# Summing the logit weights in four column groups, ordering the last two steps by hand, and idle matmuls in the last chain

## The chip, the cores and the metric

One NeuronCore of a Trainium2 chip runs the whole program. The metric is the device time of one execution in microseconds (us); the median of three executions stands in the table below. The engines are named as in the profile: PE (TensorE matmuls), PEld (TensorE weight loads), DVE (VectorE), ACT (ScalarE), POOL (GpSimd) and SP (the queue that issues the loads).

## What is computed

Three layers in a row, all in float32:

```python
attn = chunk_attention(q, k, v, mem_k, mem_v)        # 4 batches, 8 heads, 768 tokens, head size 64
x    = attn.reshape(3072, 512)
h    = x @ w_in                                      # 3072 x 2048
g    = (a0 + a1*h + a2*h^2 + a3*h^3) / (1 + |b0|*|h| + |b1|*h^2 + 1e-6)
x    = g @ w_out                                     # 3072 x 512
logits     = x @ phi                                 # 3072 x 32 slots
slot_input = softmax(logits, over tokens).T @ x      # 32 x 512, 4 slots for each of 8 experts
slot_out   = relu(slot_input[e] @ w1[e]) @ w2[e]     # each expert: 512 -> 1024 -> 512
out        = softmax(logits, over slots) @ slot_out  # 3072 x 512
```

## The kernel before

**The algebra.** `x = g @ w_out` is never formed. The logits are `g @ (w_out @ phi)`, and the kernel first makes the "logit weights" `wp = w_out @ phi` (2048 x 32). The slot input is `(softmax.T @ g) @ w_out`, so `w_out` is used once more at the end.

**Blocks and steps.** The 3072 tokens are 6 blocks of 512; a block has 8 steps of 256 features of `h`, so there are 48 steps, numbered `kk` (`total` is 48). A step's operations are written as letters in lists (`KN`), and `run_step(kk, what)` (line 558) issues one of them:

- `h0`, `h1`: the matmuls of step kk+1, two halves of 128 features by 512 tokens into a PSUM tile `h` of two banks (line 349). Block 0 multiplies in full float32; the later blocks in three products of a faster type.
- `a1`: ACT makes |b0 h| (line 576), |b1| h^2 (577) and a3 h + a2 (579); DVE adds the first two into the denominator `s` (578). `d1`: POOL refines the reciprocal of the step before (`refine`, line 553, q times w), DVE goes on with the numerator `t` (589, 590). `a2`: ACT makes a first reciprocal `w` of the denominator by Ln and Exp (595, 596). `t`: DVE finishes the step before (606, 607), which gives its `g` tile.
- `p0`, `p1`: `post` for a step two back. It turns the `g` tile on PE (line 375) and ACT copies it out of PSUM (376); in every second step `lg` accumulates the logits of two steps from `wp` (368, four column groups of 32).
- `x1` to `x3`: the softmax of a finished block (`soft1`, `soft2`, `soft3`, lines 382 to 436): the sum of the four column groups by the matrix `stack` (386, 389), maxima and Exp, the turn of the weights (416), and the product with the turned `g` tiles into `u_acc` (426, 431).
- `w1`, `z1` (block 0 alone): `wp_chunk` (line 438) turns 256 rows of `w_out` by PE and copies them out of PSUM by ACT (448) and DVE (446); `wp_sum` (line 450) makes two feature tiles of `wp` from them: for each of two tiles four matmuls over the chunks of 128 columns, with the turned `w_out` as weights (128 columns) and `phi` as the moving operand (32 columns), accumulated in PSUM (line 455), then one ACT copy (456).

The attention of block b+1 runs in slices (`at`) between the steps of block b. Block 0 also narrows `w_in` and `w_out` from their 64 bit form (`f64_narrow`, lines 300 to 304, on ACT and DVE).

**The last two steps.** Step 46 runs by the list `ordl`, step 47 by `ordz`. In step 47 the helper `parts` cuts each elementwise operation into two halves of 512 elements, so that its `g` tile comes out in halves; `refine` is on POOL there too. Two more passes (kk = 48, 49) turn the last `g` tiles; then come `soft1` to `soft3` of block 5, the turn of `u_acc` (655), the product with `w_out` (662), the sum of four groups (670), the experts' first product (683), its Relu and turn (689 to 699), the second product (720, 728) and the output.

**What sets the order.** The engines' queues are laid out by a scheduler from the order of the program and its own costs, except inside `tc.manual_schedule(engines=...)`, where the named engines keep the order that is written. `tc.issue_after(ins)` queues what its block issues behind `ins` on that engine. A queue runs strictly in order. Tiles come from pools with a fixed number of buffers: `p_S` and `p_T` (5 each, of 128 x 1024), `p_s2` (one buffer, tag "s2"), `ps_m` (three PSUM banks, taken by `bank`), `ps_h` (two tiles of two banks). A buffer is taken again when its last reader is done.

**The loads at the end.** SP loads the experts' weights (`fill`, line 536, 512 KB each) into whatever buffers come free: those of `xt` after the matmuls of step 47, those of `p_T` and `p_S` after the last steps, those of `p_g` after `soft3` of block 5, that of `p_v` after the first experts' matmuls that read it.

## Time and profile before

| | us |
|---|---|
| median of three executions | 587.33 |
| all three | 587.33, 587.27, 592.0 |
| the profiled execution | 591.32 |
| its span, first to last instruction | 589.5 |
| PE busy | 547.0 (93% of the span) |
| DVE busy | 451.8 (77%) |
| ACT busy | 413.8 (70%) |
| POOL busy | 124.3 (21%) |
| mean granted TensorE clock | 0.971 of full |

All rows come from the profiled execution, which ran about 4 us longer than the median. A busy PE is not PE at its peak, since the ends of matmuls are modelled; matmuls start one behind the other, and the distance of their starts tells what one costs. Times in the rows are us from the start of the span.

### The profile page before, as it was taken

What the parts mean: (1) busy time and instruction counts of PE and PEld (TensorE: products, weight loads), DVE (VectorE), ACT (ScalarE), POOL (GpSimd) and SP (SyncE); (2) the same over time, 40 slices, a digit from 0 to 9 for tenths busy, and PEclk for the clock granted to TensorE, in tenths of its full rate; (3) what the DMA queues carried; (4) which work ended last, traced back from release to release, by engine and by line L of the source; (5) the groups of instructions that cost most, each with busy time, mean ns of one, the idle gap of its engine ahead of it and who ended that gap; (6) DMA issues with size and microseconds to landing.
All of it is one profiled execution on the core that took longest, in us unless ns stands there. A gap on an engine that the chain in (4) does not pass through costs nothing.

```text
span 589.5 us, 13536 instructions
## 1 busy us (share of the span) xinstructions
PE 547.0 (93%) x5880; PEld 376.9 (64%) x5880; DVE 451.8 (77%) x565; ACT 413.8 (70%) x534; POOL 124.3 (21%) x65
## 2 busy tenths in 40 slices
PE   5699999999999999999999999999999999679991
PEld 5565655657767777677766777776778577237351
DVE  3668998988998989878798698896887868920132
ACT  1479997879887978769687778686888878620132
POOL 0010322212231313312231313131322333400000
PEclk9599998999999999999999999999999999898996
DMA  8879775320234312221021022210365224979949
GB/s 353 349 285 387 289 240 213 116 100 1 108 108 143 101 47 108 73 92 60 30 109 73 3 106 74 108 43 31 109 216 213 108 107 143 368 291 349 411 184 359
DMA packets 21371, 97.41 MB, mean 165 GB/s; under 512 B 2624, under 2 KB 2752, under 8 KB 16320
## 3 DMA queue, kind: packets, MB, share of 16 engines
q1 hardware_dynamic: 20160, 92.35, 42.1%
q0 software_dynamic: 1152, 4.19, 1.9%
q8 instruction: 46, 0.75, 0.5%
q14 instruction: 13, 0.11, 0.1%
HBM read 86.05 MB, written 10.49 MB: 164 GB/s over the span
## 4 chain that ended last, share of the span: by engine, by line
PE 65%; DVE 15%; ACT 10%; issue 5%; POOL 2%; DMA 1%; SPq 0%; ACTq 0%; DVEq 0%; POOLq 0%
PE h L349 32%; PE m L375 4%; PE m L426 4%; PE lg L368 3%; ACT S L576 3%; PE h L683 3%; PE m L225 2%; ACT g L376 2%; ACT S L577 2%; PE lg L720 2%; DVE T L589 2%; DVE S L578 2%; PE m L455 2%; PE m L243 2%; DVE T L590 2%
## 5 line engine op out<-in xcount | busy, mean ns | idle before, releaser
L349 PE MATMUL h<-xt,win 128*128 128x512 f32 x1024 | 268.9, 411 | 0.7 <-DVE T L590 0.6
L349 PEld LDWEIGHTS h<-xt,win 128*128 128x128 f32 x1024 | 186.1, 188 | 48.5 <-issue 10.0
L553 POOL TENSOR_TENSOR S<-S,S 128x1024 f32<-128x1024 f32 (+1 forms) x49 | 117.3, 2395 | 305.9 <-DVE S L578 287.8
L576 ACT ACTIVATE S<-h,ctab 128x1024 f32<-128x1024 f32 (+1 forms) x49 | 53.8, 1099 | 55.2 <-PE h L349 53.8
L578 DVE SCALAR_TENSOR_TENSOR S<-S,S 128x1024 f32<-128x1024 f32 (+1 forms) x49 | 58.7, 1199 | 40.4 <-ACT S L577 40.2
L606 DVE SCALAR_TENSOR_TENSOR T<-T,ctab,S 128x1024 f32<-128x1024 f32 (+1 forms) x49 | 64.8, 1324 | 0.0
L589 DVE TENSOR_TENSOR T<-T,h 128x1024 f32<-128x1024 f32 (+1 forms) x49 | 58.3, 1190 | 7.2 <-ACT T L579 7.2
L375 PEld LDWEIGHTS m<-ident,T 128*128 128x128 f32 x384 | 44.0, 143 | 30.6 <-issue 17.1
L590 DVE SCALAR_TENSOR_TENSOR T<-T,ctab,h 128x1024 f32<-128x1024 f32 (+1 forms) x49 | 61.3, 1251 | 0.8
L607 DVE SCALAR_TENSOR_TENSOR T<-S,T 128x1024 f32<-128x1024 f32 (+1 forms) x49 | 59.1, 1206 | 2.0
L579 ACT ACTIVATE T<-h,ctab 128x1024 f32<-128x1024 f32 (+1 forms) x49 | 59.2, 1208 | 0.0
L595 ACT ACTIVATE S<-S 128x1024 f32<-128x1024 f32 (+1 forms) x49 | 51.7, 1055 | 7.1 <-DVE S L578 4.9
L596 ACT ACTIVATE S<-S,ctab 128x1024 f32<-128x1024 f32 (+1 forms) x49 | 55.8, 1138 | 1.0
L376 ACT ACTIVATE g<-m 128x512 f32<-128x512 f32 x96 | 53.3, 602 | 3.4 <-PE m L375 3.2
L375 PE MATMUL m<-ident,T 128*128 128x128 f32 x384 | 53.5, 280 | 1.6 <-DVE a L186 1.6
L577 ACT ACTIVATE S<-h,ctab 128x1024 f32<-128x1024 f32 (+1 forms) x49 | 54.2, 1106 | 0.6 <-DVE T L606 0.6
L368 PE MATMUL lg<-T,wp 128*32 128x512 f32 x192 | 34.6, 612 | 4.9 <-DVE T L607 4.9
L349 PE MATMUL h<-xt,x 128*128 128x512 f32 x64 | 33.0, 635 | 0.0
L187 ACT ACTIVATE a<-a 128x512 f32<-128x512 f32 x22 | 13.7, 639 | 18.5 <-DVE a L186 18.5
L336 POOL DMA_DIRECT2D wo<-win x8 | 5.3, 666 | 84.1 <-DVE win L304 75.7
L426 PE MATMUL m<-g,s 128*32 128x512 f32 x192 | 21.8, 595 | 0.4 <-ACT s L418 0.4
L302 ACT ACTIVATE g<-g 128x1024 f32<-128x1024 f32 x16 | 18.6, 1170 | 3.5 <-DVE g L301 3.5
(172 smaller groups left out, 644.7 us busy)
## 6 DMA issues: line engine op xcount, KB each, us to landing
win<-in_moe_w_dram SPq DMA_DIRECT2D x32, 512.0 KB, 5.5
k<-in_kw_dram SPq DMA_DIRECT2D x11, 1024.0 KB, 6.0
v<-in_vw_dram SPq DMA_DIRECT2D x11, 1024.0 KB, 6.3
g<-in_moe_w_in_dram SPq DMA_DIRECT2D x8, 1024.0 KB, 7.2
g<-in_moe_w_out_dram SPq DMA_DIRECT2D x8, 1024.0 KB, 8.2
out_dram<-win SPq DMA_DIRECT2D x12, 512.0 KB, 5.0
q<-in_qw_dram SPq DMA_DIRECT2D x11, 512.0 KB, 3.6
wo<-win POOLq DMA_DIRECT2D x8, 512.0 KB, 7.7
```

The source lines that it names most:

```text
L349: PE.matmul(tile_[:, f2, :], lhsT=ww[:, c, f2 * P:f2 * P + P], rhs=xx[:, c, :], start=(n == 0), stop=(n == len(pairs) * NC - 1))
L375: PE.transpose(pb[:, m, f2 * P:f2 * P + P], t_[:, f2, tt * P:tt * P + P], ident)
L376: ACT.activation(gts[b, qd][:, 2 * part:2 * part + 2, 2 * P * o:2 * P * o + 2 * P], pb, AF.Copy)
L553: POOL.tensor_tensor(out[:, o], q[:, o], w[:, o], ALU.mult)
L576: ACT.activation(s[:, o], hh[:, o], AF.Abs, scale=b0)
L577: ACT.activation(y[:, o], hh[:, o], AF.Square, scale=rb1)
L578: DVE.scalar_tensor_tensor(s[:, o], y[:, o], QC, s[:, o], ALU.add, ALU.add)
L579: ACT.activation(t[:, o], hh[:, o], AF.Identity, bias=a2, scale=a3)
L589: DVE.tensor_tensor(t[:, o], t[:, o], hh[:, o], ALU.mult)
L590: behind[kk] = DVE.scalar_tensor_tensor(t[:, o], t[:, o], a1, hh[:, o], ALU.add, ALU.mult).ins
L606: DVE.scalar_tensor_tensor(t[:, o], t[:, o], a0, w[:, o], ALU.add, ALU.mult)
L607: DVE.scalar_tensor_tensor(t[:, o], e[:, o], 2.0, t[:, o], ALU.subtract, ALU.mult, reverse0=True)
```

## The change

Three things. First, `wp_sum` makes one product for each of the four chunks of 128 columns, with `phi` as weights (32 columns) and the turned `w_out` as moving operand (256 columns for two feature tiles), each into its own 32 PSUM partitions; ACT copies that to a tile of the pool `p_s2`; two matmuls with `stack` as moving operand then sum the four groups and turn the result in one. Second, the list `ordz` and the helper `parts` go, and `last_steps` writes out steps 46 and 47 for ACT, DVE and POOL by hand: the refinement of step 46 is cut into two halves on POOL, that of step 47 is on DVE, the finish of step 46 stands behind the first part of step 47, and the ACT copies of step 45's turned tile stand between the two halves of Ln and Exp. Third, `keep_busy` issues matmuls of the identity with itself (128 x 128 float32) into a PSUM tile that nobody reads, queued behind given matmuls: 5 in `soft1`, 2 in `soft3`, 19 in `last_steps` (the last 7 read `w`), 2 after the turn of `u_acc`, 3 after the product with `w_out`.

```diff
-    'ordz': "d0 a1 t d1 a2 p0 p1".split(),
     'ordl': "a1 h0 d1 t a2 x2 h1 p0 p1 x1 x3".split(),
 }
 
@@ -372,7 +371,7 @@
         for m in range(2):
             for f2 in range(2):
                 tt = 2 * part + m
-                PE.transpose(pb[:, m, f2 * P:f2 * P + P], t_[:, f2, tt * P:tt * P + P], ident)
+                st["turn"] = PE.transpose(pb[:, m, f2 * P:f2 * P + P], t_[:, f2, tt * P:tt * P + P], ident)
         ACT.activation(gts[b, qd][:, 2 * part:2 * part + 2, 2 * P * o:2 * P * o + 2 * P], pb, AF.Copy)
         if part and o:
             del gt_tile[k - 1], gt_tile[k]
@@ -386,7 +385,9 @@
         PE.matmul(lt, lhsT=stack, rhs=lgs, start=True, stop=True)
         ct = bank([P, TT, NSLOT])
         for tt in range(TT):
-            PE.matmul(ct[:, tt, :], lhsT=lgs[:, tt * P:tt * P + P], rhs=stack[:, 0:NSLOT], start=True, stop=True)
+            done = PE.matmul(ct[:, tt, :], lhsT=lgs[:, tt * P:tt * P + P], rhs=stack[:, 0:NSLOT], start=True, stop=True)
+        if b == NBLK - 1:
+            keep_busy(done.ins, 5)
         old, neg_m = (run[:, n:n + 1] for n in ((2, 0) if b % 2 else (0, 2)))
         bm, db = p_sm("bm", [P, 1]), p_sm("db", [P, 1])
         DVE.tensor_reduce(bm, lt, AX.X, ALU.max)
@@ -432,7 +433,9 @@
         for j in range(4):
             del gts[b, j]
         pb = bank([P, P])
-        PE.transpose(pb, ce.rearrange("p t s -> p (t s)"), ident)
+        done = PE.transpose(pb, ce.rearrange("p t s -> p (t s)"), ident)
+        if b == NBLK - 1:
+            keep_busy(done.ins, 2)
         ACT.activation(c_all[:, b, :], pb, AF.Copy)
 
     def wp_chunk(i):
@@ -448,11 +451,15 @@
                 ACT.activation(ws[:, j], pb, AF.Copy)
 
     def wp_sum(i):
+        ws = wos.pop(i)
+        pb = bank([P, 2, P])
+        for c in range(NC):
+            PE.matmul(pb[32 * c:32 * c + 32], lhsT=phi_sb[:, c, :], rhs=ws[:, :, c, :], start=True, stop=True)
+        part = p_s2("s2", [P, 2, P])
+        ACT.activation(part, pb, AF.Copy)
         pb = bank([P, 2, NSLOT])
-        ws = wos.pop(i)
         for j in range(2):
-            for c in range(NC):
-                PE.matmul(pb[:, j, :], lhsT=ws[:, j, c, :], rhs=phi_sb[:, c, :], start=(c == 0), stop=(c == NC - 1))
+            PE.matmul(pb[:, j, :], lhsT=part[:, j, :], rhs=stack[:, 0:NSLOT], start=True, stop=True)
         ACT.activation(wp[:, 2 * i:2 * i + 2, :], pb, AF.Copy)
 
     xtra = [p_xt("xt", [P, 2048]) for _ in range(2)]
@@ -543,14 +550,10 @@
 
     LATER = [(2,), (2,), (), (3, 2), (2,), (2,), (2,), (2,)]
 
-    def parts(kk):
-        return [slice(n, n + 1) for n in range(2)] if kk == total - 1 else [slice(0, 2)]
-
     def refine(k, out=None):
         t, q, w = late[k]
         near[k] = out = q if out is None else out
-        for o in parts(k):
-            POOL.tensor_tensor(out[:, o], q[:, o], w[:, o], ALU.mult)
+        POOL.tensor_tensor(out, q, w, ALU.mult)
 
     late, near, behind = {}, {}, {}
     act = {}
@@ -572,11 +575,10 @@
         elif what == "a1" and live:
             hh = hs[kk]
             s, t, y = p_S("S", [P, 2, BLK]), p_T("T", [P, 2, BLK]), p_S("S", [P, 2, BLK])
-            for o in parts(kk):
-                ACT.activation(s[:, o], hh[:, o], AF.Abs, scale=b0)
-                ACT.activation(y[:, o], hh[:, o], AF.Square, scale=rb1)
-                DVE.scalar_tensor_tensor(s[:, o], y[:, o], QC, s[:, o], ALU.add, ALU.add)
-                ACT.activation(t[:, o], hh[:, o], AF.Identity, bias=a2, scale=a3)
+            ACT.activation(s, hh, AF.Abs, scale=b0)
+            ACT.activation(y, hh, AF.Square, scale=rb1)
+            DVE.scalar_tensor_tensor(s, y, QC, s, ALU.add, ALU.add)
+            ACT.activation(t, hh, AF.Identity, bias=a2, scale=a3)
             act[kk] = s, t, y
         elif what == "d1":
             if live:
@@ -585,26 +587,21 @@
             if kk - 1 in late and kk - 1 not in near:
                 refine(kk - 1, y if nxt < total else None)
             if live:
-                for o in parts(kk):
-                    DVE.tensor_tensor(t[:, o], t[:, o], hh[:, o], ALU.mult)
-                    behind[kk] = DVE.scalar_tensor_tensor(t[:, o], t[:, o], a1, hh[:, o], ALU.add, ALU.mult).ins
+                DVE.tensor_tensor(t, t, hh, ALU.mult)
+                behind[kk] = DVE.scalar_tensor_tensor(t, t, a1, hh, ALU.add, ALU.mult).ins
         elif what == "a2" and live:
             s, t, _ = act.pop(kk)
             w = p_S("S", [P, 2, BLK])
-            for o in parts(kk):
-                ACT.activation(w[:, o], s[:, o], AF.Ln, scale=2.0 ** -LN_SHIFT)
-                st["exp"] = ACT.activation(w[:, o], w[:, o], AF.Exp, bias=ex_b, scale=-1.0).ins
+            ACT.activation(w, s, AF.Ln, scale=2.0 ** -LN_SHIFT)
+            st["exp"] = ACT.activation(w, w, AF.Exp, bias=ex_b, scale=-1.0).ins
             late[kk] = t, s, w
-        elif what == "d0":
-            refine(kk - 1)
         elif what == "t":
             if kk - 1 in late:
                 t, q, w = late.pop(kk - 1)
                 e = near.pop(kk - 1)
                 with tc.issue_after(behind[kk]) if kk in behind else nullcontext():
-                    for o in parts(kk - 1):
-                        DVE.scalar_tensor_tensor(t[:, o], t[:, o], a0, w[:, o], ALU.add, ALU.mult)
-                        DVE.scalar_tensor_tensor(t[:, o], e[:, o], 2.0, t[:, o], ALU.subtract, ALU.mult, reverse0=True)
+                    DVE.scalar_tensor_tensor(t, t, a0, w, ALU.add, ALU.mult)
+                    DVE.scalar_tensor_tensor(t, e, 2.0, t, ALU.subtract, ALU.mult, reverse0=True)
                 gt_tile[kk - 1] = t
         elif what == "y":
             if 0 <= kk - 6 < NSTEP:
@@ -621,6 +618,50 @@
         elif b == 0 and what[0] in "snwzio" and len(what) == 2:
             convert(what[0] + str(min(i + int(what[1]), NSTEP)))
 
+    idle = {}
+
+    def keep_busy(ins, n, rhs=None):
+        if "t" not in idle:
+            idle["t"] = ps_h("h", [P, 2, BLK])
+        with tc.issue_after(ins):
+            for _ in range(n):
+                PE.matmul(idle["t"][:, 0, 0:P], lhsT=ident, rhs=ident if rhs is None else rhs, start=True, stop=True)
+
+    def last_steps():
+        k, z = total - 2, total - 1
+        for what in "a1 h0 d1 p0 p1 t a2 h1".split():
+            run_step(k, what)
+        hh = hs.pop(z)
+        s, t, y = p_S("S", [P, 2, BLK]), p_T("T", [P, 2, BLK]), p_S("S", [P, 2, BLK])
+        w = p_S("S", [P, 2, BLK])
+        t_, q_, w_ = late.pop(k)
+        for n in range(2):
+            o = slice(n, n + 1)
+            ACT.activation(s[:, o], hh[:, o], AF.Abs, scale=b0)
+            ACT.activation(y[:, o], hh[:, o], AF.Square, scale=rb1)
+            ACT.activation(t[:, o], hh[:, o], AF.Identity, bias=a2, scale=a3)
+            DVE.scalar_tensor_tensor(s[:, o], y[:, o], QC, s[:, o], ALU.add, ALU.add)
+            POOL.tensor_tensor(y[:, o], q_[:, o], w_[:, o], ALU.mult)
+            DVE.tensor_tensor(t[:, o], t[:, o], hh[:, o], ALU.mult)
+            DVE.scalar_tensor_tensor(t[:, o], t[:, o], a1, hh[:, o], ALU.add, ALU.mult)
+        for n in range(2):
+            o = slice(n, n + 1)
+            ACT.activation(w[:, o], s[:, o], AF.Ln, scale=2.0 ** -LN_SHIFT)
+            ACT.activation(w[:, o], w[:, o], AF.Exp, bias=ex_b, scale=-1.0)
+            if n == 0:
+                for part in range(2):
+                    post(k - 1, part)
+                keep_busy(st["turn"].ins, 12)
+                keep_busy(st["turn"].ins, 7, w[:, 0, 0:P])
+        DVE.scalar_tensor_tensor(t_, t_, a0, w_, ALU.add, ALU.mult)
+        DVE.scalar_tensor_tensor(t_, y, 2.0, t_, ALU.subtract, ALU.mult, reverse0=True)
+        for n in range(2):
+            o = slice(n, n + 1)
+            DVE.tensor_tensor(s[:, o], s[:, o], w[:, o], ALU.mult)
+            DVE.scalar_tensor_tensor(t[:, o], t[:, o], a0, w[:, o], ALU.add, ALU.mult)
+            DVE.scalar_tensor_tensor(t[:, o], s[:, o], 2.0, t[:, o], ALU.subtract, ALU.mult, reverse0=True)
+        gt_tile[k], gt_tile[z] = t_, t
+
     for kk in range(total + 4):
         b, i = divmod(kk, NSTEP)
         if kk == last:
@@ -632,8 +673,12 @@
             fill(p_xt, "xt", 2, 2)
         if i == 0 and b < NBLK - 1:
             state["att"] = attention_block(b + 1)
-        for what in KN["ord0" if b == 0 else "ord" if b < NBLK - 1 else "ordz" if kk == total - 1 else "ordl"]:
-            run_step(kk, what)
+        if kk == total - 2:
+            with tc.manual_schedule(engines={ACT.engine, DVE.engine, POOL.engine}):
+                last_steps()
+        elif kk != total - 1:
+            for what in KN["ord0" if b == 0 else "ord" if b < NBLK - 1 else "ordl"]:
+                run_step(kk, what)
         if last <= kk < total:
             fill(p_win, "win", 2, 1)
         if kk == total - 1:
@@ -652,16 +697,18 @@
 
     pb = bank([P, 4, P])
     for n in range(4):
-        PE.transpose(pb[:, n, :], u_acc[:, n * P:n * P + P], ident)
+        done = PE.transpose(pb[:, n, :], u_acc[:, n * P:n * P + P], ident)
+    keep_busy(done.ins, 2)
     ut = p_s2("s2", [P, 4, P])
     ACT.activation(ut, pb, AF.Copy)
     pb = bank([P, DM])
     for n in range(4):
         for j in range(4):
             ft = 4 * j + n
-            PE.matmul(pb[32 * j:32 * j + 32, :], lhsT=ut[:, n, 32 * j:32 * j + 32],
-                      rhs=w_out_rows(ft),
-                      start=(n == 0), stop=(n == 3))
+            done = PE.matmul(pb[32 * j:32 * j + 32, :], lhsT=ut[:, n, 32 * j:32 * j + 32],
+                             rhs=w_out_rows(ft),
+                             start=(n == 0), stop=(n == 3))
+    keep_busy(done.ins, 3)
     fill(p_v, "v", 1, 2)
     si = p_s2("s2", [P, DM])
     ACT.activation(si, pb, AF.Copy, scale=rden)
```

## Rows read from the trace of the kernel before

**Rows 1.** Page, part 2: the span in 40 slices of 14.7 us, tenths.

```profile
PEclk9599998999999999999999999999999999898996
DMA  8879775320234312221021022210365224979949
```

**Rows 2.** Windows, block 0: busy us of PE, PEld, DVE, ACT, POOL; clock, DMA, GB/s.

```profile
40.00:60.00 20.00, 20.00 (x216) 12.71 (x214) 17.80 (x26) 18.30 (x22) 2.56 (x3) 1.00 0.97 369
60.00:80.00 20.00, 18.63 (x239) 12.03 (x238) 20.00 (x22) 17.71 (x22) 4.35 (x3) 1.00 0.78 284
...
sum 100.00, PE 97.06 PEld 60.60 DVE 90.89 ACT 84.79 POOL 21.36; mean PE 19.41 PEld 12.12 DVE 18.18 ACT 16.96 POOL 4.27
```

**Rows 3.** Chain of waits, 40 to 140 us, shares by line.

```profile
by line: PE h L349 32.6%; PE m L455 11.1%; DVE win L304 5.5%; DVE g L301 4.7%; PE m L375 4.5%; DVE x L304 3.8%; PE m L444 3.7%; DVE S L578 3.5%; DVE T L589 3.0%; issue 3.0%; DVE T L590 2.4%; ACT g L302 2.3%; ACT S L576 2.1%; ACT g L300 2.1%
```

**Rows 4.** Groups of 40 to 140 us: busy, mean ns, idle before and releaser.

```profile
L455 PE MATMUL m<-u,S 128*128 128x32 f32 x128 | 15.7, 273 | 1.9 <-DVE S L446 1.9
```

**Rows 5.** Timeline (start us, us, engine line): prices for the new `wp_sum`.

```profile
42.22 1.87 PE L455 MATMUL m<-u,S 128*128 128x32 f32 x16
...
479.35 1.06 PE L368 MATMUL lg<-T,wp 128*32 128x512 f32 x8
...
480.34 1.53 PE L375 MATMUL m<-ident,T 128*128 128x128 f32 x12
...
566.74 0.39 ACT L733 ACTIVATE u<-lg 128x256 f32<-128x256 f32 x1 [10.86 <-PE lg L728]
```

**Rows 6.** Chain of waits in order of time, the experts' products.

```profile
533.97 10.79 PE h L683 x80
...
555.25 9.58 PE lg L720 x88
564.82 1.89 PE lg L728 x32
```

**Rows 7.** Timeline of the last two steps, DVE, ACT and POOL.

```profile
498.88 2.41 POOL L553 TENSOR_TENSOR S<-S,S 128x1024 f32<-128x1024 f32 x1 [4.53 <-DVE S L578]
501.25 3.33 POOL L553 TENSOR_TENSOR S<-S,S 128x1024 f32<-128x1024 f32 x1
...
499.90 1.28 DVE L590 SCALAR_TENSOR_TENSOR T<-T,ctab,h 128x1024 f32<-128x1024 f32 x1
501.10 1.28 DVE L606 SCALAR_TENSOR_TENSOR T<-T,ctab,S 128x1024 f32<-128x1024 f32 x1
502.30 3.37 DVE L606 SCALAR_TENSOR_TENSOR T<-T,ctab,S 128x1024 f32<-128x1024 f32 x1
508.46 0.68 DVE L578 SCALAR_TENSOR_TENSOR S<-S,S 128x512 f32<-128x512 f32 x1
515.31 0.69 DVE L607 SCALAR_TENSOR_TENSOR T<-S,T 128x512 f32<-128x512 f32 x1
...
501.32 0.69 ACT L576 ACTIVATE S<-h,ctab 128x512 f32<-128x512 f32 x1 [0.31 <-POOL S L553]
501.91 1.08 ACT L376 ACTIVATE g<-m 128x512 f32<-128x512 f32 x2
...
511.04 1.27 POOL L553 TENSOR_TENSOR S<-S,S 128x512 f32<-128x512 f32 x1 [6.45 <-ACT S L596]
```

**Rows 8.** Windows of 2 us in the last chain, columns as in rows 2.

```profile
508.00:510.00 2.00, 2.00 (x9) 1.46 (x8) 1.97 (x4) 0.44 (x2) 0.00 (x0) 0.50 1.03 418
...
524.00:526.00 2.00, 1.98 (x18) 0.40 (x9) 0.13 (x1) 0.00 (x0) 0.00 (x0) 1.00 0.02 8
...
534.00:536.00 2.00, 2.00 (x12) 1.69 (x16) 0.48 (x6) 0.00 (x0) 0.00 (x0) 0.60 1.03 418
536.00:538.00 2.00, 2.00 (x15) 1.68 (x11) 0.00 (x0) 0.00 (x0) 0.00 (x0) 0.55 0.81 332
538.00:540.00 2.00, 2.00 (x24) 1.88 (x20) 0.00 (x0) 0.00 (x0) 0.00 (x0) 1.00 0.65 203
```

**Rows 9.** Line 728: what its weight loads waited for (us, times).

```profile
  DMA T<-in_moe_w_dram: 0.4, 1
```

## The prediction

> **What bounds the kernel now.** I read the page's slices first, then windows, then the chain of waits and the timeline in the two places that the change touches. The slices show one program with several limits [rows 1]. The TensorE clock digit is 9 nearly everywhere; after the first 30 us it is 8 in one slice of block 0 (88 to 103 us) and in two late ones (from 500 and from 530 us), and the DMA digits are back at 9 only at the late end. So the middle (blocks 1 to 5) is left as it is: nothing of the change runs in it. Two regions count: block 0, where `wp_sum` runs, and the last chain, from about 494 us on.
>
> Block 0: between 40 and 140 us PE is busy for 97.1 us of 100, DVE for 90.9, ACT for 84.8 [rows 2]. Three engines are nearly full; PE is the fullest, and in 60 to 80 us DVE is (20.00 of 20.00, PE 18.63). The chain of waits through this stretch gives 32.6% to the matmuls of `h` (line 349) and 11.1% to line 455, the matmuls of `wp_sum`; lines of DVE stand in it too [rows 3]. So line 455 is on the path for 11.1 us, but an engine that is almost as full stands behind it.
>
> Last chain: until `soft1` can start, DVE works without a pause, and two places are slow. One `t` operation (606) takes 3.37 us where the one before it took 1.28 [rows 7]. It has two operands in SBUF, and it starts while POOL's refinement of step 46 runs (501.25 to 504.58); it ends about one operation later than that. Line 590, whose `h` operand is in PSUM, ran its usual 1.28 us beside an earlier POOL operation [rows 7]. After that the experts' products run on PE with loads beside them; PE's clock is 1.2 GHz in 508 to 510, and its mean is 0.60 and 0.55 in 534 to 538 [rows 8]; ahead of that second fall stands the chain of 655, 662 and 670, each behind a DVE or ACT operation. The very last load is waited for, 0.4 us [rows 9]: PE and loads end together.
>
> **`wp_sum`.** Before: 16 matmul records a call, 1.87 us by the timeline [rows 5], some 0.11 us each, 128 records in eight calls [rows 4]. After, first product: four float32 matmuls are eight records of 256 columns in four column groups. The nearest rows are line 728's, 32 records of the same shape in 1.89 us [rows 6]: eight make 0.47. Second product: two matmuls, four records of the old shape: 0.47 by line 455's rate. Going into column groups and back costs something: line 368's eight records of 512 columns are two groups of four, 0.87 us by line 720's rate (88 records in 9.58 us), but the next kind of matmul starts 0.99 us after the first of them [rows 5, 6], so 0.12 us at the way out; as much again is my estimate for the way in, 0.24 together. New: 0.47 + 0.47 + 0.24 = 1.18, against 1.87: 0.69 us less a call, 0.65 after a small margin, and 5.2 us of PE for eight calls. The Trainium skill, TensorEngine Tiling (Array Packing), section Key Properties, speaks against the change here: changing the tiling mode drains the array. The trace agrees, with the 0.12 us at the way out. By the rule alone without that row I would have no figure; without the drain the sum would be 1.9 us better for eight calls.
>
> Added beside it: one ACT copy of 128x256 a call, 0.39 us [rows 5], 3.1 us in all on an engine with 15 us free in the stretch [rows 2]; one more PSUM bank of three and the single `s2` buffer, both held for about a microsecond. The second product needs that copy; what hides the wait is the other PE work of the step, the matmuls of `h` above all. If that cover is gone, PE stands for the copy and what ACT does ahead of it.
>
> How much of 5.2 us shortens block 0? Bounds: all 5.2 if PE sets every call's place; none if DVE takes over (its slack is 9 us in 100). I take five of eight: 60 to 80 us is DVE's, and PE waited 1.9 us for the DVE copy (446) ahead of line 455 [rows 2, 4], a wait that stays, since the first product now needs both copies. 5 x 0.65 = 3.2 us. Below nothing: the second product as a stall (a rival below).
>
> **The last two steps by hand.** From the start of step 45's last pair on DVE (501.10 [rows 7]) the written order gives DVE four full operations (606, 607 of steps 45 and 46) and twelve halves: six of step 47's first part, six of its last, the refinement among them. At 1.2 us from start to start for the full (501.10 to 502.30) and 0.66 for halves, an estimate just under their 0.68 [rows 7], that is 4.8 + 7.9 = 12.7, so 513.8. POOL's two halves (1.27 each) start when the denominators' halves are done, beside operations that read `h` from PSUM; the second still meets the start of step 46's 606, and I add 0.1. Before, the end was 515.31 + 0.69 = 516.0 [rows 7]. So 2.1 us earlier. ACT has to follow: first half at about 502.0, behind step 46's Exp (it was 501.32 [rows 7]); six halves of 0.6, Ln and Exp 1.3, two copies 1.08, Ln and Exp 1.3 end at 509.3; the halves of `w` are wanted at 509.9 and 511.9. PE follows with 19 idle matmuls of two records each, 0.11 us a record as other 128-wide loads of weights cost: 4.2 us, between the turns of step 45 (about 505) and step 46's tile (509.9). The last seven wait for the first half of `w` (507.0), and behind them stand step 46's turns, which have no tile before 509.9. Bounds: the old order put ACT's two copies of step 43's tile (1.08 us, the shape of 501.91 [rows 7]) between step 46's 576 and 577; if they go behind, DVE starts that much earlier and the gain is 3.2 us, if they are forced ahead it is 1.0.
>
> Queues: the loads into `xt` need the end of step 47's matmuls, and the turns of step 44 may now stand between its two halves, 0.9 us; loads run back to back there, and the DMA pause at 524 to 526 (share 0.02 [rows 8]) takes that up.
>
> **Idle matmuls.** In `soft1`, `soft3`, behind 655 and 662 they are 5, 2, 2 and 3 (0.4 to 1.1 us), each in a gap where PE waits for DVE or ACT; I cost them at nothing, up to 0.3 us each if a gap is shorter. What they can save: 534 to 538 ran at 0.60 and 0.55, so (0.40 + 0.45) x 2 = 1.7 us were lost. (Bounds: nothing, or 2.1: the 80 records from 533.97 took 10.79 us, and at the later rate of 88 in 9.58 it would be 8.7 [rows 6].) The loads must follow. Their idle share of 536 to 540 is 2 x 0.19 + 2 x 0.35 = 1.1 us [rows 8], because the buffers come free late there; with faster PE that goes, and nothing more is sure. I take 1.5 of 1.7.
>
> **Sum.** Against the profiled execution (591.32, a span of 589.5 and 1.8 around it): 3.2 + 2.1 + 1.5 = 6.8, so 584.5. The median is 4.0 below that execution, and the profile has two stretches of half clock that an execution of the median may lack (the digit 8 in block 0 [rows 1], and the one at 534). I credit the median with half of the clock's term, 0.8: 587.33 - 3.2 - 2.1 - 0.8 = 581.2 us.
>
> **Rivals.**
> - More: PE sets all eight calls, and the median has the slow stretch too: 587.33 - 5.2 - 2.1 - 1.5 = 578.5. For it: PE 20.00 of 20.00 in the first window [rows 2]. Against: DVE's 20.00 in the second.
> - Block 0 keeps its length: DVE and ACT hold it. 587.33 - 2.1 - 0.8 = 584.4. For it: DVE 90.9 of 100. Against: line 455's 11.1%.
> - The idle matmuls don't hold the clock, so that this part doesn't do what it says, or the median never lost it. For it: 2 to 3 matmuls in gaps that are longer than they are. 587.33 - 3.2 - 2.1 = 582.0. Against: PE's clock stayed full through the gaps around 524 to 526 us [rows 8].
> - Slower: the second product stands in PE's queue behind nothing else, eight times, and waits for an ACT copy that is itself behind one of ACT's full operations (1.1 to 1.2 us). Then PE waits some 1.6 us a call and gains 0.65: 0.95 x 8 = 7.6, so 587.33 + 7.6 - 2.9 = 592.0. It outweighs the rest from a wait of about 1.0 us a call (0.65 + 2.9 / 8). For it: line 455 did wait for copies before. Against: matmuls of `h` are ready at nearly all times.
>
> **How the numbers follow.** Forecast 0.45 (own range 579 to 583.5), more 0.22, block 0 unchanged 0.15, clock not held 0.10, slower 0.08. The range 576.5 to 586.0 leaves out the slower case and the ends. One per cent, about what a measurement of this kernel can tell from no change, is 5.9 us: faster by more means below 581.46. That is 0.25 of the forecast's 0.45, all of "more" and 0.03 of the clock's case: 0.50. Slower by more (over 593.2): half of the slower case and a little: 0.05. The rest, 0.45, is within.
>
> **What would show it.** Right: line 576's first operation of block 1 some 3 us earlier; second products of `wp_sum` with no wait of PE ahead of them; no `t` operation over 1.5 us after 500; the last 607 about 12.7 us after step 45's 606; clock 1.00 from the last step to the last expert product; the experts' products about 30 us long. Wrong: PE waiting for ACT's new copies; DVE full and PE no longer so in block 0 with the same length; PE waiting for loads in the second expert product; idle matmuls ahead of work that is ready.

## The result, and the profile after

The changed kernel took 583.46 us (median of four executions, 582.38 to 585.57); the kernel before took 589.66 beside it (587.27 to 592.26). The ratio is 0.9895, with an interval of 0.9856 to 0.9934: 6.2 us less, give or take 2.3. (The 587.33 in the table above is the median of three of the executions of before; the fourth, 592.26, moves it to 589.66.) Forecast were 6.1 less, counted from 587.33, and a time of 581.2. The sum was right within the measurement; its split was not, as the runs show.

The page of the profiled execution after (583.87 us, a span of 582.1), parts 1 and 2, beside [rows 1]:

```profile
PE 542.7 (93%) x5910; PEld 369.7 (64%) x5910; DVE 447.2 (77%) x567; ACT 415.4 (71%) x542; POOL 121.4 (21%) x64
...
PEclk9799999999999999999999999999999999999996
DMA  8889874401135303231032111320374423989939
```

The clock digit is 9 from 30 us on until the output; the three 8s of before are gone.

Block 0 of the kernel after by windows, beside [rows 2]:

```profile
40.00:60.00 20.00, 19.16 (x205) 9.34 (x204) 17.84 (x27) 19.62 (x26) 3.93 (x3) 1.00 1.01 388
60.00:80.00 20.00, 18.85 (x262) 10.59 (x261) 19.97 (x22) 19.57 (x26) 4.00 (x3) 1.00 0.73 260
...
sum 100.00, PE 95.10 PEld 52.57 DVE 92.29 ACT 91.27 POOL 22.52; mean PE 19.02 PEld 10.51 DVE 18.46 ACT 18.25 POOL 4.50
```

Its groups of 40 to 140 us for the new sum, beside [rows 4] (457 the first product, 462 the second, 459 the copy between them; PEld is the weight loads):

```profile
L457 PE MATMUL m<-S,u 128*32 128x256 f32 x64 | 5.1, 390 | 1.4 <-DVE S L449 1.3
L462 PEld LDWEIGHTS m<-stack,s 128*128 128x128 f32 x32 | 4.6, 190 | 6.8 <-ACT s L459 5.4 <-issue 1.2
L462 PE MATMUL m<-stack,s 128*128 128x32 f32 x32 | 4.5, 265 | 1.9 <-ACT s L459 1.9
L459 ACT ACTIVATE s<-m 128x256 f32<-128x256 f32 x8 | 3.1, 385 | 0.1
```

PE is no longer full in the first window, and ACT went from 84.8 to 91.3 of 100 (the window of after holds 4.5 us of block 1, too). The two products keep PE busy for 5.1 + 4.5 = 9.6 us where line 455 took 15.7 [rows 4]; part of the 6.1 came back as waiting for the new copy (line 459). Its cost on ACT, 0.39 a call, is the forecast's.

Block 0 alone, from the first Abs of step 0 to that of step 8, in a kernel with the old sum that ran it at full clock (the one with the 12 idle matmuls alone, below), and in the kernel after:

```profile
39.76:137.65 97.89, 95.00 (x930) 59.28 (x929) 90.65 (x103) 85.53 (x104) 22.04 (x14) 1.00 0.58 211
39.84:135.54 95.70, 90.80 (x898) 49.05 (x897) 88.30 (x103) 87.17 (x113) 22.52 (x14) 1.00 0.59 216
```

PE is busy for 4.2 us less and idle for 4.9 instead of 2.9 us: the block is 2.2 us shorter.

The timeline of the last two steps after, DVE (beside [rows 7]; 640 to 646 are the first part of step 47, 603 and 604 finish step 45, 656 and 657 step 46, 662 is the last operation of step 47):

```profile
493.54 1.28 DVE L603 SCALAR_TENSOR_TENSOR T<-T,ctab,S 128x1024 f32<-128x1024 f32 x1
494.93 1.23 DVE L604 SCALAR_TENSOR_TENSOR T<-S,T 128x1024 f32<-128x1024 f32 x1
...
497.39 0.75 DVE L646 SCALAR_TENSOR_TENSOR T<-T,ctab,h 128x512 f32<-128x512 f32 x1
499.47 0.69 DVE L643 SCALAR_TENSOR_TENSOR S<-S,S 128x512 f32<-128x512 f32 x1 [1.33 <-ACT S L641]
...
507.44 0.69 DVE L662 SCALAR_TENSOR_TENSOR T<-S,T 128x512 f32<-128x512 f32 x1
```

and ACT beside it:

```profile
495.75 0.78 ACT L642 ACTIVATE T<-h,ctab 128x512 f32<-128x512 f32 x1
498.18 0.69 ACT L640 ACTIVATE S<-h,ctab 128x512 f32<-128x512 f32 x1 [1.64 <-DVE T L646]
```

No operation of line 603 or 656 is over 1.28 us now, as forecast. But from the start of 603 to the end of the last 662 it is 14.6 us and not the 12.7 of the sum: ACT's second half waits 1.64 us for DVE's last reader (646) of the first half, and DVE then pauses 1.33 for ACT.

To compare kernels I took the time between the starts of the same operations from each trace. "Block 0" runs from the first Abs of step 0 to that of step 8, "3 and 4" from that of step 24 to step 40, "last steps" from that of step 46 to the end of the last operation 607 (662 after), "to max" from there to `soft1`'s maximum, "softmax" on to the last update of `u_acc`, "experts" from their first product to the copy of the second one's result, "output" from there to the end.

| us | block 0 | 3 and 4 | last steps | to max | softmax | experts | output |
|---|---|---|---|---|---|---|---|
| before | 99.65 | 153.84 | 21.62 | 2.95 | 6.91 | 32.77 | 22.81 |
| after | 95.70 | 152.22 | 21.30 | 2.95 | 6.92 | 33.17 | 22.82 |
| after, a second execution | 95.77 | 152.21 | 21.29 | 2.95 | 6.91 | 30.98 | 22.83 |
| after, a third execution | 95.55 | 152.27 | 21.31 | 2.95 | 6.92 | 30.97 | 22.79 |
| new sum alone | 95.72 | 152.37 | 21.86 | 2.95 | 8.61 | 33.00 | 24.16 |
| hand order alone | 97.91 | 154.27 | 21.31 | 3.26 | 8.62 | 33.05 | 22.84 |
| 12 idle matmuls alone | 97.89 | 152.88 | 20.74 | 2.95 | 6.92 | 33.21 | 22.81 |
| after, no idle matmuls | 95.73 | 152.26 | 21.30 | 3.94 | 6.92 | 31.40 | 24.19 |
| the same, padded | 95.76 | 153.75 | 21.31 | 4.05 | 6.92 | 31.77 | 22.83 |
| after, without the 19 | 95.65 | 152.21 | 21.30 | 3.58 | 6.92 | 33.54 | 22.81 |
| after, the 19 alone | 95.72 | 152.21 | 21.30 | 2.95 | 8.32 | 31.34 | 22.80 |
| after, order put back | 95.67 | 152.35 | 21.85 | 2.95 | 6.92 | 31.45 | 22.82 |
| after, ACT first | 95.73 | 152.25 | 21.53 | 3.57 | 6.92 | 31.30 | 22.82 |
| after, own bank | 95.71 | 152.21 | 19.81 | 2.95 | 7.08 | 32.01 | 22.81 |

Each row is one profiled execution. Ahead of the first Abs three executions of the changed kernel need 39.8, 39.7 and 42.2 us, with a mean clock of 0.91, 0.87 and 0.88 there; no part of the change is in that stretch, and the clock does not order the three times.

### The profile page after: what moved, and what is told of

Read it like the earlier page. It is cut to its first block, busy times and chain, and to the rows that moved or that the text cites. A ratio compares the mean times of both kernels' runs of the same rounds, so it can differ in the third digit from the quotient of the medians.

```text
span 582.1 us, 13606 instructions
## 1 busy us (share of the span) xinstructions
PE 542.7 (93%) x5910; PEld 369.7 (64%) x5910; DVE 447.2 (77%) x567; ACT 415.4 (71%) x542; POOL 121.4 (21%) x64
## 4 chain that ended last, share of the span: by engine, by line
PE 55%; DVE 14%; ACT 13%; DMA 9%; issue 3%; POOL 2%; SPq 0%; ACTq 0%; POOLq 0%; DVEq 0%
PE h L348 30%; PE m L374 5%; PE m L427 4%; PE lg L367 3%; ACT S L578 3%; DMA win<-in_moe_w_dram 3%; ACT S L579 3%; POOL S L556 2%; PE m L224 2%; DMA g<-in_moe_w_in_dram 2%; DMA g<-in_moe_w_out_dram 2%; DVE T L591 2%; ACT g L375 2%; DMA T<-in_moe_w_dram 2%; DVE S L580 2%
## 5 line engine op out<-in xcount | busy, mean ns | idle before, releaser
L556 POOL TENSOR_TENSOR S<-S,S 128x1024 f32<-128x1024 f32 x46 | 111.5, 2423 | 298.5 <-DVE S L580 298.5
L578 ACT ACTIVATE S<-h,ctab 128x1024 f32<-128x1024 f32 x47 | 52.4, 1114 | 50.2 <-PE h L348 48.9
L580 DVE SCALAR_TENSOR_TENSOR S<-S,S 128x1024 f32<-128x1024 f32 x47 | 57.4, 1222 | 37.6 <-ACT S L579 37.3
L590 DVE TENSOR_TENSOR T<-T,h 128x1024 f32<-128x1024 f32 x47 | 57.0, 1213 | 6.8 <-ACT T L581 6.6
L591 DVE SCALAR_TENSOR_TENSOR T<-T,ctab,h 128x1024 f32<-128x1024 f32 x47 | 59.9, 1274 | 0.8
L603 DVE SCALAR_TENSOR_TENSOR T<-T,ctab,S 128x1024 f32<-128x1024 f32 x46 | 58.6, 1274 | 0.0
L604 DVE SCALAR_TENSOR_TENSOR T<-S,T 128x1024 f32<-128x1024 f32 x46 | 56.2, 1221 | 2.2
L581 ACT ACTIVATE T<-h,ctab 128x1024 f32<-128x1024 f32 x47 | 57.5, 1223 | 0.0
L596 ACT ACTIVATE S<-S,ctab 128x1024 f32<-128x1024 f32 x47 | 54.4, 1158 | 0.9
L595 ACT ACTIVATE S<-S 128x1024 f32<-128x1024 f32 x47 | 50.4, 1073 | 6.0 <-DVE S L580 3.3
L579 ACT ACTIVATE S<-h,ctab 128x1024 f32<-128x1024 f32 x47 | 52.7, 1120 | 0.6 <-DVE T L603 0.6
```

What stands on the lines that cost most here:

```text
L556: POOL.tensor_tensor(out, q, w, ALU.mult)
L578: ACT.activation(s, hh, AF.Abs, scale=b0)
L579: ACT.activation(y, hh, AF.Square, scale=rb1)
L580: DVE.scalar_tensor_tensor(s, y, QC, s, ALU.add, ALU.add)
L581: ACT.activation(t, hh, AF.Identity, bias=a2, scale=a3)
L590: DVE.tensor_tensor(t, t, hh, ALU.mult)
```

## The experiments

**Each part alone.** Into the kernel before went the hunk of `wp_sum` alone, the hunks of the last two steps without `keep_busy`, and the 12 idle matmuls of `soft1`, `soft3` and the two later products; the fourth is the changed kernel with every call of `keep_busy` out.

```diff
+            PE.matmul(pb[32 * c:32 * c + 32], lhsT=phi_sb[:, c, :], rhs=ws[:, :, c, :], start=True, stop=True)
...
+        if kk == total - 2:
+            with tc.manual_schedule(engines={ACT.engine, DVE.engine, POOL.engine}):
+                last_steps()
...
+            keep_busy(done.ins, 5)
...
-                keep_busy(st["turn"].ins, 12)
```

> The kernel before with the new wp_sum alone. By the prediction's term: 3.2 us faster (ratio 0.9945), PE-bound calls five of eight. By the rival 'block 0 keeps its length': no change (0.999 to 1.001). By the rival of the second product standing in PE's queue: slower, and PE waiting for ACT's copy in the rows of the second product. By the comparison of the two traces: block 0 (first operation of block 1 less that of block 0) was 95.7 us against 99.7, but 4.1 of it in one step where the kernel before ran at half clock; so 2 to 4 us.

> The kernel before with the last two steps by hand alone, without idle matmuls. By the prediction: 2.1 us faster (0.9964). By the trace of the changed kernel: ACT's first operation on the second half waited 1.6 us for the DVE operation on the first half, so the last 607 comes only 0.3 to 0.5 us earlier than before, measured from the 576 of step 46; 0.9985 to 1.000.

> The kernel before with the idle matmuls of soft1, soft3 and behind 655 and 662 alone (12 matmuls; those of the last steps have no place here). If the clock's fall at 534 costs its 1.7 us: 0.8 to 1.7 us faster (0.997 to 0.9985) and the clock full through the experts' products. If the experts' products end with their loads whatever PE does: no change within 0.5 us, the clock full, and PE waiting for loads at the last product for as long as it gained.

> The changed kernel without any idle matmul. If the loads set the end: the same as the changed kernel within 0.5 us (ratio to before 0.989 to 0.991), with a stretch at half clock in some of its executions and less waiting for loads. If the idle matmuls carry part of the gain: 0.8 to 2 us slower than the changed kernel (0.991 to 0.993).

Measured against before: new sum 0.9942 (0.9918 to 0.9966), hand order 1.0014 (0.9982 to 1.0046), idle matmuls 0.9967 (0.9944 to 0.9990), all but idle matmuls 0.9949 (0.9925 to 0.9972). The new sum alone gives 3.4 us (2.0 to 4.8), the hand order nothing that can be told (1.1 us less to 2.7 more; its trace has a stretch at half clock in `soft3`, 8.62 us, which the profile of before lacks, so that up to 1.7 us may be hidden there). Block 0 is 95.6 to 95.8 in every kernel with the new sum and 97.9 in the two that have the old one at full clock: 2.2 us. (The profile of before has 99.65, with a half-clock stretch from 90.7 on.) In blocks 3 and 4, which the change does not touch, kernels with the old sum need 152.9 to 154.3, those with the new one 152.2 to 152.4, but the padded one.

The kernel without idle matmuls shows where they count. Windows of it (columns as in [rows 2]):

```profile
504.00:506.00 2.00, 0.00 (x0) 0.00 (x0) 1.89 (x3) 1.97 (x4) 0.05 (x1) 0.86 1.02 412
506.00:508.00 2.00, 1.18 (x6) 1.21 (x7) 1.97 (x4) 0.21 (x2) 0.00 (x0) 0.50 1.03 420
508.00:510.00 2.00, 2.00 (x10) 0.57 (x8) 1.97 (x4) 1.14 (x2) 0.00 (x0) 0.50 1.03 416
510.00:512.00 2.00, 2.00 (x6) 0.47 (x4) 0.66 (x1) 0.00 (x0) 0.00 (x0) 0.50 1.04 416
```

PE stood idle from 504 to 506, the granted clock fell to 0.50 (1.2 GHz), and the turn and logits behind the last DVE operation took 3.94 us instead of 2.95. The expectation's other outcome, the same time as the changed kernel, is out: 0.9949 against 0.9861 to 0.9895.

**The written order.** First ACT's six operations of step 47 ahead of DVE's, beside the changed kernel once more:

```diff
             ACT.activation(t[:, o], hh[:, o], AF.Identity, bias=a2, scale=a3)
+        for n in range(2):
+            o = slice(n, n + 1)
             DVE.scalar_tensor_tensor(s[:, o], y[:, o], QC, s[:, o], ALU.add, ALU.add)
```

> The changed kernel with ACT's six operations of step 47 (both halves of Abs, Square, Identity) written ahead of DVE's on either half. If ACT's wait of 1.6 us for DVE's operation on the first half is an order that the listing made: no such wait, DVE's pause of 1.3 us ahead of the second denominator gone, the last 607 about 1.3 us earlier from the 576 of step 46 (20.0 against 21.3). At the end 1.3 us faster than the changed kernel if the loads into the freed g buffers start earlier by that, 0 if the loads ahead of them hold them. By the rival (ACT must wait for the same PSUM tile in any order): nothing changes.

> The changed kernel as it is, timed beside the three others of this call. If the idle matmuls are worth what the last call suggests: a ratio to before of 0.988 to 0.991, against 0.995 without any.

Measured: 0.9892 (0.9864 to 0.9919) against 0.9874 (0.9847 to 0.9902) for the changed kernel. The wait moved over to DVE and stayed as long; the last steps took 21.53 us, not the 20.0 that were expected if the listing alone made the wait. (Behind them the clock was at 0.69 and 0.50 from 505 to 509 us, and the first maximum came 0.6 us later.) DVE's timeline in the kernel with ACT first:

```profile
496.05 0.68 DVE L645 SCALAR_TENSOR_TENSOR S<-S,S 128x512 f32<-128x512 f32 x1
498.37 0.69 DVE L647 TENSOR_TENSOR T<-T,h 128x512 f32<-128x512 f32 x1 [1.64 <-ACT T L642]
```

So it looks like a wait between the two engines that read one PSUM tile, and it goes by the order in which the program names them: the first half's multiply has all of its data at 496.5, and waits for ACT's last operation on the second half. Then the sharing was taken away, with the second half of step 47's `h` in a bank of its own:

```diff
-        for what in "a1 h0 d1 p0 p1 t a2 h1".split():
+        for what in "a1 h0 d1 p0 p1 t a2".split():
             run_step(k, what)
-        hh = hs.pop(z)
+        own = bank([P, 1, BLK])
+        h_part(z, None, 1, own[:, 0, :])
+        halves = hs.pop(z)[:, 0:1], own
...
```

> The changed kernel with the second half of step 47's matmuls in a PSUM tile of its own (one of the three of ps_m) instead of the second bank of the shared tile h. If the wait of ACT for DVE comes from the shared PSUM tile: ACT's first operation on the second half starts behind its last on the first half, at about 8.9 us after the 576 of step 46 instead of 11.4, DVE doesn't pause, and the last 607 comes 1.2 us earlier (20.1 against 21.3). The loads into the freed g buffers then start 1.2 us earlier and the whole is about 1.2 us faster (0.998 of the changed kernel). If something else holds ACT: 21.3 as before. If the borrowed bank holds the turns of steps 44 and 45 up: PE waiting for ACT's copies, and the gain is smaller.

> The changed kernel as it is, beside these two on the same chip: the base of both. The part of the experts' products took 33.2 us in one execution and 31.0 in another; a third tells which is usual.

Measured: 581.5 us and 0.9845 (0.9801 to 0.9889), the changed kernel beside it 582.99 and 0.9861 (0.9819 to 0.9904). ACT's timeline with the own bank:

```profile
495.65 0.77 ACT L644 ACTIVATE T<-h,ctab 128x512 f32<-128x512 f32 x1
496.31 0.69 ACT L642 ACTIVATE S<-m,ctab 128x512 f32<-128x512 f32 x1
```

and DVE's:

```profile
497.41 0.75 DVE L648 SCALAR_TENSOR_TENSOR T<-T,ctab,h 128x512 f32<-128x512 f32 x1
498.07 0.68 DVE L645 SCALAR_TENSOR_TENSOR S<-S,S 128x512 f32<-128x512 f32 x1
...
505.96 0.69 DVE L664 SCALAR_TENSOR_TENSOR T<-S,T 128x512 f32<-128x512 f32 x1
```

Neither wait is left; the stretch is 19.81 us instead of 21.30. The halves lay in two banks before as well, and the tiles in SBUF that both engines use (`s`, `t`, `y`) are shared as before; the tile of `h` is what the run took apart. Of the two totals the intervals overlap; the 1.5 us of the stage are in the traces, and the medians differ by as much.

Last, the order of before inside the changed kernel, with the new sum and the 12 idle matmuls (the lines that bring `ordz`, `parts` and the old operations back are left out):

```diff
...
-        if kk == total - 2:
-            with tc.manual_schedule(engines={ACT.engine, DVE.engine, POOL.engine}):
-                last_steps()
-        elif kk != total - 1:
-            for what in KN["ord0" if b == 0 else "ord" if b < NBLK - 1 else "ordl"]:
-                run_step(kk, what)
+        for what in KN["ord0" if b == 0 else "ord" if b < NBLK - 1 else "ordz" if kk == total - 1 else "ordl"]:
+            run_step(kk, what)
```

> The changed kernel with the order of the last two steps put back as it was (the lists, parts, POOL for both refinements) and without the 19 idle matmuls that belong to the written order; the new sum of the logit weights and the 12 idle matmuls in soft1, soft3 and behind the two products stay. My theory (the written order gained nothing: DVE lost as much by the refinement that it took over and by its pause as the clash with POOL had cost): the last 607 stands 20.7 to 21.6 us behind the first Abs of step 46 (21.30 with the written order), block 0 is 95.7, and the ratio lies between 0.986 and 0.991, as that of the changed kernel (0.986 to 0.9895 in three comparisons). Rival (the written order is worth the forecast's 2.1 us, and it was hidden when it was tried alone, since there the clock was low behind it): the last 607 stands over 23 us behind that Abs and the ratio is 0.991 or more. A third reading, by adding what the parts gave alone (0.9942 and 0.9967): 0.991 with no loss in the last steps, the difference to the changed kernel being the clock or the loads behind them.

Measured: 582.96 us, 0.9883 (0.9854 to 0.9912), no different from the changed kernel. Its last steps take 21.85, 0.55 more than the written order, so that the rival (over 23 us, and a ratio of 0.991 or more) is out; the third reading's 0.991 lies at the edge of the interval. The clash with POOL is back, in DVE's timeline (614 and 615 are 606 and 607 of before):

```profile
494.22 4.57 DVE L614 SCALAR_TENSOR_TENSOR T<-T,ctab,S 128x1024 f32<-128x1024 f32 x2
...
506.14 1.74 DVE L615 SCALAR_TENSOR_TENSOR T<-S,T 128x512 f32<-128x512 f32 x1 [0.51 <-POOL S L561]
```

and in POOL's:

```profile
492.00 5.71 POOL L561 TENSOR_TENSOR S<-S,S 128x1024 f32<-128x1024 f32 x2 [4.54 <-DVE S L586]
504.32 3.01 POOL L561 TENSOR_TENSOR S<-S,S 128x512 f32<-128x512 f32 x2 [6.61 <-DVE T L597]
```

**Which idle matmuls.** The changed kernel without the 19 of the last steps (the edit shown), and with these alone (the calls with 5, 2, 2 and 3 out):

```diff
-                keep_busy(st["turn"].ins, 12)
-                keep_busy(st["turn"].ins, 7, w[:, 0, 0:P])
```

> The changed kernel without the 19 idle matmuls of the last steps. By the clock: PE may be at 1.2 GHz when step 47's tile comes, 1.0 us between the last 607 and the first maximum (3.9 against 2.95). By the place of instruction loads: the last load of PE's instructions, 559.7 in the changed kernel, comes 76 instructions later, beside the output's transfers, and the time from the sum of the experts' products to the end is 24.2 instead of 22.8 us. Together 1 to 2.4 us slower than the changed kernel.

> The changed kernel with the 19 idle matmuls of the last steps alone. By the clock: a stretch at 1.2 GHz somewhere from soft1 to the experts' first product; 1.7 us if it falls on the product of soft3, as in two of the runs so far, nothing if it falls on the experts' products (which took 32.8 to 33.2 us with it and without it). By the place of instruction loads: 48 instructions later, still ahead of the output's transfers, so the end part stays at 22.8. 0 to 1.7 us slower than the changed kernel.

Measured: 0.9922 (0.9893 to 0.9950) without the 19, 0.9939 (0.9915 to 0.9962) with them alone, 0.9874 for all in the same comparison. Without the 19 the median is 3.0 us longer, with them alone 3.8; the traces show 0.6 for the 19 (3.58 to 2.95) and 1.4 for those of `soft1` and `soft3` (8.32 to 6.92). With the 19 alone the clock falls in the products into `u_acc`, by windows of that kernel:

```profile
513.00:515.00 2.00, 0.98 (x8) 0.52 (x12) 1.03 (x6) 1.02 (x4) 0.00 (x0) 0.72 1.02 406
515.00:517.00 2.00, 2.00 (x12) 0.39 (x8) 0.00 (x0) 0.00 (x0) 0.00 (x0) 0.50 0.67 262
```

What the medians show beyond this is not settled; the experts and the prelude vary more than that from one execution to another. One expectation failed: without the 19 the last load of PE's instructions was to fall beside the output's transfers and lengthen it to 24.2 us. It came at 565.6, ahead of the first of them, and the output took 22.81.

**The end of the output.** The two kernels with 24.2 us of output both have PE's last instruction load (one 16 KB packet, at 569.9 and 571.4 us) beside the output transfers; in the twelve other traces it lies ahead of the first of them. The twelve outputs land 1.2 to 1.4 us apart in those twelve traces; in these two the second lands 1.9 and the third 2.6 us behind the one before it. 32 small matmuls at the start of block 3, in the kernel without idle ones, shift where that load falls:

```diff
+        if kk == 3 * NSTEP:
+            pad = bank([P, 2 * P])
+            for m in range(32):
+                g = 32 * (m % 4)
+                PE.matmul(pad[g:g + 32, 0:32], lhsT=ident[0:32, 0:32], rhs=ident[0:32, 0:32], start=True, stop=True)
```

> The changed kernel without idle matmuls, with 32 small matmuls of 32 columns (64 records) at the start of block 3, where PE runs at full clock: about as many instructions of PE as the idle matmuls, none of them near the last chain. If the place of the instruction load sets the length of the output part: the last load of PE's instructions comes ahead of the output's transfers, near 560 instead of 569.9 us, and that part takes 22.8 us instead of 24.2. If the idle matmuls' effect there was the clock: still 24.2. In both cases the first maximum comes late by up to 1.0 us as without idle matmuls, and the small matmuls cost up to 1 us.

Measured: 0.9938 (0.9900 to 0.9976) where it was 0.9949, no difference to be told in the total; but the load now falls at 561.3, ahead of the output transfers, and the output takes 22.83. The DMA queues from 568 to 574 us without the pad (packets, MB, share of 16 engines):

```profile
q1 hardware_dynamic: 655, 2.39, 100.9%
q8 instruction: 1, 0.02, 1.0%
```

and what SP waited for at its end (us, times, longest):

```profile
SPq L857 <- DMA out_dram<-win: 5.0, 4, 1.4
```

With the pad only the loads' and outputs' own queue has packets in the window:

```profile
q1 hardware_dynamic: 671, 2.43, 102.0%
```

and SP's waits are shorter by the 1.3 us of one transfer:

```profile
SPq L862 <- DMA out_dram<-win: 3.7, 3, 1.3
```

So a load that falls there is shown to cost the output 1.36 us; that it is one of PE's instructions follows from its moving with matmuls that were added far ahead. The 1.36 us went into blocks 3 and 4 (152.26 to 153.75), of which the added matmuls are 0.75.

## Why the prediction was right or wrong

**`wp_sum`: right in sum (-3.2, measured -3.4), partly by luck.** Block 0 became 2.2 us shorter, not 3.2. PE is busy for 4.2 us less there, where 5.2 were forecast (the records of the sum alone fell by 6.1; why the two differ is not shown), and 2.0 of that came back as waiting. The wrong step is "what hides the wait is the other PE work": PE's matmuls waited 1.9 us for the copy ahead of the second products, 0.24 a call, and the weight loads before them 5.4, 0.68 a call. The rival of a slower kernel is this mechanism; its point of 1.0 us a call was not reached. The wait before the first product stayed in kind (1.4 us, was 1.9). That the new sum alone measures 3.4 and not 2.2 is within its interval. Where the traces show more, it is in blocks 3 and 4 (152.4 us against 152.9 to 154.3), of which I had said that nothing of the change runs there; the new sum alone then lost 1.35 at the output. That both follow from where PE's instruction loads fall, since the new sum has fewer matmuls, is shown for the output by the pad; for blocks 3 and 4 it is argued, and the pad's loss there fits it.

**The last two steps: wrong (-2.1, measured nothing).** The clash of POOL with 606 was read rightly and is gone, 2.1 us for the longest operation. But from 603 (606 before) to the end it is 14.6 us, and was 14.9. The step that failed is ACT's: "six halves of 0.6" were run together, where the second three stand behind DVE's readers of the same tile. DVE's pause for it is 1.33 us; with the own bank the same operations take 13.1, 0.4 more than the 12.7, and most of that remainder is the full operations' distance (2.53 us a pair, estimated 2.4). Nor was the end of before a fixed thing to count from: its order took 20.74 to 21.86 us in four kernels, against 21.30 for the written one. It loses to POOL, but it has the refinement of step 47 off DVE (2 x 0.68 us), and DVE pauses less (0.51 us in the kernel with the order put back).

The Trainium skill, SBUF — State Buffer, section Who interferes with whom, says that a DVE instruction with two SBUF inputs contends with a GpSimd instruction that reads SBUF, over a port pair that one of them locks. The trace agrees: two of line 614 take 4.57 us beside POOL's 5.71, and 1.28 each in the written order. The rule says nothing of the PSUM tile, whose readers set the end.

**Idle matmuls: the clock was held; the loads followed in two of three executions, and more was saved elsewhere.** The forecast had them save 1.5 us in the experts' products, 0.8 of it for the median, and nothing in other places. That they hold the clock is borne out: between the first maximum and the end of the experts' products none of the eight traces with the 12 has a stretch at half clock, and four of the six without them have one. (The row that was cited for it, 524 to 526 us [rows 8], shows PE busy for 1.98 of 2 us; PE's gaps stand beside it.) "The loads must follow" held in part. In the three kernels whose clock falls in the experts' first product, the loads pause right behind it: a DMA share of 0.81 and 0.65 before [rows 8], and in the new sum alone

```profile
533.00:535.00 2.00, 2.00 (x23) 1.60 (x19) 0.00 (x0) 0.00 (x0) 0.00 (x0) 0.97 0.21 47
```

At the same distance from the first product, the kernel after has no such pause, nor have the ten other traces at full clock:

```profile
528.00:530.00 2.00, 2.00 (x25) 1.78 (x20) 0.00 (x0) 0.00 (x0) 0.00 (x0) 1.00 1.04 381
530.00:532.00 2.00, 2.00 (x24) 1.80 (x20) 0.00 (x0) 0.00 (x0) 0.00 (x0) 1.00 0.94 350
```

That the buffers coming free late makes the pause, as the forecast says, fits this and is not tested by itself. The stage took 32.8 to 33.1 us with the pause. Without it, it took 31.0 to 32.0 in eight traces (31.0 in two of the changed kernel), but 33.2 to 33.5 in three, the changed kernel's first among them. In these three the last loads landed late though they had not paused; in all fourteen traces the stage ends within 1.0 us of the last landing. What line 775, the experts' last products, waited for in the first execution of the changed kernel (us, times):

```profile
  DMA win<-in_moe_w_dram: 2.9, 5
  DMA T<-in_moe_w_dram: 1.7, 2
```

and in a second execution of it:

```profile
  issue: 0.6, 2
  DMA T<-in_moe_w_dram: 0.3, 1
```

What makes the loads land late in some executions (33.17 and 30.98 us are the same kernel) stays open. The stage also ran at full clock with no idle matmul at all (31.40), after the clock had been low earlier. The step that was missing is what the idle matmuls save ahead of the experts, put at nothing: 1.0 us behind the last step and 1.4 to 1.7 in `soft3`. Alone the 12 give 0.9967, some 1.9 us; in the changed kernel all 31 give 0.9861 to 0.9895 in three comparisons, against 0.9949 without them, 3.2 to 5.2 us, of which 1.36 are the output's, by the instruction load and not by the clock.

**The sum.** Three terms of 3.2, 2.1 and 0.8 were forecast; shown are 3.4, about 0 and 1.9 alone or 3.2 to 5.2 in place. That the total came out at 6 is luck: two errors of opposite sign. Of the signs named beforehand, the full clock from the last step on came in all three executions and experts near 30 us in two; PE waiting for the new copies, a sign of being wrong, came too. The own range, 579 to 583.5, held the 583.46 by little. The rivals "clock not held" at 582.0 and "block 0 keeps its length" at 584.4 lay nearer to it than the forecast's 581.2, for the wrong reasons: the clock was held, and block 0 got shorter.

## What to carry to other kernels

Before an elementwise stage is cut into halves by hand, see that the halves lie in tiles of their own: two engines that read one PSUM tile follow each other in program order, and here that took back what the new order had gained. A matmul that saves PE time by a copy in between is paid by the wait for that copy, so count it by call. Keep PE running where PE's own work ends the stage next; where loads end it, the clock is worth what it spares the loads, here a pause of 1.1 to 1.6 us (an estimate from the idle shares), and an execution whose loads land late for another reason shows nothing of it.

## What was not expected of the hardware

One instruction load of PE, a single packet of 16 KB, beside the output transfers made the output 1.35 us longer (24.2 instead of 22.8 in the two kernels where it fell there, 22.8 in the others), and adding 32 tiny matmuls 280 us earlier moved it away. The Trainium skill, DMA: Bandwidth & Descriptors, section Queues, rings and completion order, says that a DMA engine takes turns between its queues by whole packets; that fits one engine's share of a transfer landing late, but no run here shows the engine's own order. The 27 late loads of 512 KB that follow `soft3` took 38.2 to 41.0 us from the first issue to the last landing in the traces. In the three with the pause it was 40.3 to 40.5; the others spread over the whole range, and the changed kernel's three executions took 40.7, 38.5 and 38.2.
